# LayerNorm of the second row pair by ScalarE's square root, and another split of FFN1's blocks over the first two pairs

## The chip, the cores and the metric

The kernel runs on one core of one Trainium2 chip. The metric is the device time of one execution in microseconds. The kernel before takes 165.26 us, the median of 3 runs (164.93 to 165.86).

## The reference

The kernel adds two branches to its input. Both read the same LayerNorm of x. Branch A is a linear attention with softmax features, 16 heads of 28; branch B is a feed-forward net with SiLU.

```python
S, D, H, Dh, F = 2048, 448, 16, 28, 1792
xn = (x - mean(x)) / sqrt(var(x) + 1e-5)                    # per row
q, k, v = split_heads(xn @ wqkv)
pq, pk = q @ w_phi, k @ w_phi                                # per head, 28 x 28
phi_q = concat(softmax(pq), softmax(-pq)); phi_k = concat(softmax(pk), softmax(-pk))
kv = phi_k^T v;  z = sum over rows of phi_k
a = merge_heads((phi_q @ kv) / (phi_q . z + 1e-6)) @ wo
b = silu(xn @ w1) @ w2                                       # w1 448 x 1792, w2 1792 x 448
out = x + a + b
```

## The kernel before, in words

**Tiles.** The 2048 rows are 16 tiles of 128 rows, worked on in 8 pairs of tiles. A pair's normalised rows go through TensorE transposes into `xnT`, which every later matmul contracts over. FFN1 (`xn @ w1`, then SiLU) is cut into 14 blocks of 128 of the 1792 hidden columns.

**Who writes the order.** The program is a list of operations (`P.op`, `P.dma`) with their reads and writes. `schedule()` (lines 218 to 330) orders them per engine with planned durations, priorities and order-only edges (`odeps`). Each engine then runs its own list strictly in that order and waits on semaphores (`emit_engine`, line 1022). So an instruction that waits holds up all that stand behind it on its engine.

**LayerNorm.** `ln_stats` (589) takes mean and variance of a tile on VectorE. For pair 0, `ln_pair_first` (623) has ScalarE take the square root (629, tile `std`) and VectorE the reciprocal (632); `ln_norm` (601) normalises; `ln_tr` (610) transposes on TensorE and evicts PSUM to `xnT`, three of seven column blocks on ScalarE and four on VectorE. Between these stand warm-up matmuls on an identity matrix (528). For the other pairs, `ln_pair` (651) uses `ln_rstd` (595): VectorE adds epsilon (598) and GpSimd takes the power -0.5 (599); all seven blocks are evicted in one copy on VectorE (467). For pair 1 the two tiles have a power of their own each (`one_by_one`).

**ScalarE's tables.** The square root needs one table of functions, SiLU another. The compiler puts a table load ahead of the first instruction that needs another table.

**FFN1.** `ffn1_chunk(p0, npair, f0, fend, units)` (667) computes blocks f0 to fend for npair pairs that start at p0. One chunk fills two PSUM banks: four blocks of one pair (matmuls 128 wide) or two blocks of two pairs (256 wide). `contract` (472) makes two passes over each chunk: four steps of two matmuls that run side by side in the upper and lower half of the rows, then three steps with the halves exchanged; the second pass waits until the first is done. A chunk ends with a SiLU on ScalarE (688) that empties its two banks. `units` names the first bank of each chunk in turn; a chunk on banks that an earlier one used waits for that one's SiLU.

**The start.** Lines 737 to 764: pair 0's and pair 1's LayerNorm, blocks 0 to 10 of pair 0 alone (chunks of 4, 4, 3), pair 2's LayerNorm, the same blocks of pair 1 alone, pair 3's, then blocks 11 to 13 of both, pair 4's, and blocks of pairs 2 and 3 together. After FFN1 of six pairs and the folding of `w_phi` into the q and k weights come the k, v and q projections, the state kv, and the output with FFN2; FFN1 of pairs 6 and 7 fills in at a lower priority (963).

**Loads.** SP's queue carries, in order: x of tile 0, w1's first part, x of tiles 2 and 3, w1's second part (three transfers), w1's third part (three transfers, 557 to 562), x of pair 2, x of pair 3. The later loads are paced: x of tiles 8 to 11, wqkv and others each wait for one of the evictions to `xnT` (983 to 985).

Of the kernel before, what the change touches and what calls it, by code (L numbers as in the profile page):

```python
# [7 lines left out]
F32 = mybir.dt.float32  # L8
ACTF = mybir.ActivationFunctionType
# [323 lines left out]
def bass_parallel_sum__linear_kernel_hedgehog__dense_activation_silu__prompt_kernel(  # L333
# [13 lines left out]
    FT = FF // 128  # L347
# [7 lines left out]
    with es:  # L355
        def sb(name, shape, dt):
            return es.enter_context(nc.sbuf_tensor(name, shape, dt))
# [27 lines left out]
        ones4 = sb("ones4", [128, 4], F32)  # L385
        pre = sb("pre", [128, 2], F32)
        epsc = sb("epsc", [128, 1], F32)
        std = sb("std", [128, 2], F32)
        mtmp2 = sb("mtmp2", [128, 4], F32)
        mtmp3 = sb("mtmp3", [128, 4], F32)  # L390
        mask2 = sb("mask2", [128, 2], F32)
# [1 line left out]
        mv = sb("mv", [128, NT, 2], F32)  # L393
        ve = sb("ve", [128, NT], F32)
        neghalf = sb("neghalf", [128, NT], F32)
# [22 lines left out]
        P = _Prog()  # L418
# [43 lines left out]
        def act(dst, src, func, name, table=None, scale=1.0):  # L462
            return P.op("act", d_act(_cols(src)), lambda e: e.activation(dst, src, func, scale=scale),  # L463
                        reads=[src], writes=[dst], table=table, name=name)
# [7 lines left out]
        def contract(jobs, n, first, last, name, sync=None):  # L472
# [6 lines left out]
            for q, steps in enumerate(passes):  # L479
# [21 lines left out]
             reads=[ones_bf[:]], writes=[ident[:]], name="ident")  # L501
# [1 line left out]
        P.op("pool", d_pool(4), lambda e: e.memset(ones4[:], 1.0), writes=[ones4[:]], name="ones4")  # L503
        P.op("pool", d_pool(280, 0.9), lambda e: e.memset(BD[:], 0.0), writes=[BD[:]], name="bd0")
        P.op("pool", d_pool(1), lambda e: e.memset(epsc[:], EPS_LN), writes=[epsc[:]], name="eps")
        pre_op = act(pre[:, 0:1], neghalf[:, 0:1], ACTF.Sqrt, "pre", scale=-1.0)

        def late_constants():
            v4 = [a[:].rearrange("p (j h) -> p j h", j=2) for a in (ones4, mtmp2, mtmp3)]
# [16 lines left out]
             name="wopad")  # L526
# [14 lines left out]
        def load_x(t0, t1, eng="sp"):  # L541
            return load(x_sb[:, t0:t1, :], xt[:, t0:t1, :], (t1 - t0) * 128 * D * 2, f"x{t0}", eng)
# [17 lines left out]
        for c0, c1 in ((512, 1024), (1024, FF)):  # L560
            load_k(w1_sb, B_w1, c0, c1, "w1b")
            load_tail(w1_sb, B_w1, c0, c1, "w1bt")
        load_x(4, 6)
        load_x(6, 8)
        first_loads = len(P.ops)
        paced = []
# [34 lines left out]
        def ln_norm(p, t, eng="dve"):  # L601
            sl = p % NXN
            for c0, c1, o0 in (((0, D, 0),) if t % 2 == 0 else ((384, D, D), (0, 384, 512))):
                xn = xn_sb[:, sl, o0:o0 + c1 - c0]
                dur = 120 + (c1 - c0) * 0.6 if eng == "dve" else 120 + (c1 - c0) * 1.0
                P.op(eng, dur, lambda e, xn=xn, c0=c0, c1=c1: e.tensor_scalar(
                    xn, x_sb[:, t, c0:c1], mv[:, t, 0:1], rstd[:, t:t + 1], ALU.subtract, ALU.mult),
                    reads=[x_sb[:, t, c0:c1], mv[:, t, 0:1], rstd[:, t:t + 1]], writes=[xn], name="xn")
# [11 lines left out]
            else:  # L620
                copy_dve(dst, src, "xnT_ev", d_dve(128 * n, 2))

        def ln_pair_first(bk):
            for t in range(2):
                k = len(P.ops)
                ln_stats(t)
                if t:
                    P.ops[k].odeps.add(k - 2)
                P.op("act", 220, lambda e, t=t: e.activation(std[:, t:t + 1], mv[:, t, 1:2], ACTF.Sqrt, bias=epsc[:]),
                     reads=[mv[:, t, 1:2], epsc[:]], writes=[std[:, t:t + 1]], name="std")  # L630
            for t in range(2):
                P.op("dve", 150, lambda e, t=t: e.reciprocal(rstd[:, t:t + 1], std[:, t:t + 1]),
                     reads=[std[:, t:t + 1]], writes=[rstd[:, t:t + 1]], name="rstd")
                ln_norm(0, t)
            prev = None
            for n, js, eng in ((19, [0, 1, 2], "act"), (2, [3, 4, 5, 6], "dve")):
                k = len(P.ops)
                o = warm(n, 256)
                if prev:
                    P.ops[k].odeps.add(prev)  # L640
                k = len(P.ops)
                ln_tr(0, js, bk if eng == "act" else bk - 2, eng)
                P.ops[k].odeps.add(o.id)
                prev = P.ops[-1].id - 1
            ev = P.ops[-1]
            k = len(P.ops)
            o = warm(5, 256)
            P.ops[k].odeps.add(prev)
            return ev, o

        def ln_pair(p, one_by_one=False):
            t0, t1 = 2 * p, 2 * p + 1
            for t in (t0, t1):
                ln_stats(t)
                if one_by_one:
                    ln_rstd(t, t + 1)
            if not one_by_one:
                ln_rstd(t0, t1 + 1)
            ln_norm(p, t0)
            ln_norm(p, t1)  # L660
            ln_tr(p, [0, 1, 2, 3, 4, 5, 6], 6, "dve")

        silus = []
# [72 lines left out]

        last0, warm0 = ln_pair_first(6)
        k = len(P.ops)
        ln_pair(1, True)
        for o in P.ops[k:]:  # L740
            if o.eng == "dve":
                o.odeps.add(last0.id)
# [1 line left out]
        k = len(P.ops)  # L744
        ffn1_chunk(0, 1, 0, 4, (0, 2))
        P.ops[k].odeps.add(warm0.id)
        ffn1_chunk(0, 1, 4, 8, (0, 2))
        ffn1_chunk(0, 1, 8, 11, (0, 2))
        k = len(P.ops)
        ln_pair(2)  # L750
        for o in P.ops[k:]:
            if o.eng == "dve":
                o.odeps.add(last1)
        ffn1_chunk(1, 1, 0, 4)
        ffn1_chunk(1, 1, 4, 8)
        ffn1_chunk(1, 1, 8, 11)
        ln_pair(3)
        ffn1_chunk(0, 2, 11, FT)
        ln_pair(4)
        ffn1_chunk(2, 2, 0, 4)  # L760
        ln_pair(5)
# [219 lines left out]
            else:  # L981
                out_last(p)
        evs = [o.id for o in P.ops if o.name == "xnT_ev"]
        for o, d in zip(paced, evs[2:6]):
            o.deps.add(d)
        eks = [o.id for o in P.ops if o.name == "exp_k"]
        for o, d in zip(w2_loads + [wo_load], eks[0::2]):
# [112 lines left out]
```

## Time and profile before

| | us |
|---|---|
| median of 3 runs | 165.26 |
| lowest, highest | 164.93, 165.86 |
| the profiled execution | 165.84 |
| its span (first to last instruction) | 164.1 |
| TensorE busy / VectorE / ScalarE / GpSimd | 158.3 / 102.3 / 73.8 / 54.5 |
| granted TensorE clock | 1.0 all along |

The profile shows one execution. PE is TensorE's matmuls, PEld its weight loads, which run beside them; DVE is VectorE, ACT ScalarE, POOL GpSimd, SP SyncE. A row of a timeline has start, length, engine, line, operation, output and inputs, and how many like it were merged; in brackets stand the idle time of the engine ahead of it and what ended that. Matmuls are pipelined and their ends are modelled.

### The profile page before, as it was taken

The page shows a single profiled execution, that of the slowest core. Times are in us where ns is not written, and L with a number is a line of the kernel's source. Part 1 is how long each engine was busy: PE and PEld are TensorE (multiplying, and loading weights), DVE is VectorE, ACT ScalarE, POOL GpSimd, SP SyncE. Part 2 cuts the span into 40 slices and gives each one's busy share as a digit, 9 for nine tenths or more (in the row PEclk, how much of TensorE's full clock was granted, in tenths as well). Part 3 has the DMA queues.
Part 4 walks back from the last instruction along what each step waited for, and adds up shares of the span by engine and source line. Part 5 has one row for each costly group of instructions (what it writes and reads, how often), then busy time and mean ns, then how long its engine had stood idle before and what let it go on. Part 6 is the DMA issues. An engine that isn't in the chain of part 4 may idle for free.

```text
span 164.1 us, 5978 instructions
## 1 busy us (share of the span) xinstructions
PE 158.3 (96%) x2741; PEld 102.7 (63%) x2741; DVE 102.3 (62%) x185; ACT 73.8 (45%) x85; POOL 54.5 (33%) x79
## 2 busy tenths in 40 slices
PE   6999999999999999999999999999999999999994
PEld 4689799999754455545557865555555554455563
DVE  2859878932418887666878788578867865111211
ACT  3542756569688866786667562210220131200000
POOL 7021130110001777755574052553464265000000
PEclk9999999999999999999999999999999999999999
DMA  5974743000003332120000000010101010101011
GB/s 162 311 202 116 203 129 108 0 4 4 4 0 112 116 112 60 46 72 4 4 4 6 0 4 4 0 56 4 50 10 56 0 60 2 56 3 56 0 62 50
DMA packets 8197, 9.24 MB, mean 56 GB/s; under 512 B 1324, under 2 KB 7916, under 8 KB 8172
## 3 DMA queue, kind: packets, MB, share of 16 engines
q1 hardware_dynamic: 7868, 8.62, 17.1%
q8 instruction: 21, 0.34, 0.8%
q10 hardware_dynamic: 304, 0.25, 0.5%
q14 instruction: 4, 0.03, 0.1%
HBM read 7.02 MB, written 1.84 MB: 54 GB/s over the span
## 4 chain that ended last, share of the span: by engine, by line
PE 83%; DVE 7%; DMA 3%; ACT 2%; SPq 2%; issue 1%; DVEq 0%; ACTq 0%
PE psum L444 47%; PE psum L438 33%; PE psum L457 3%; DMA w_sb<-in_B_w_dram 3%; DVE scr L798 2%; SPq L536 2%; DVE wraw L901 1%; DVE Sk L795 1%; ACT oT L463 1%; ACT scr L463 1%; DVE den L892 1%; DVE KVZ L854 1%; DVE kvt L849 0%; DVE R L888 0%; DVE rden L895 0%
## 5 line engine op out<-in xcount | busy, mean ns | idle before, releaser
L444 PE MATMUL psum<-xnT,w_sb 64*128 64x256 bf16 (+1 forms) x938 | 49.4, 252 | 1.0 <-DMA w_sb<-in_B_w_dram 0.6
L438 PE MATMUL psum<-w_sb,hT 128*128 128x448 bf16 (+2 forms) x238 | 47.1, 342 | 0.0
L444 PEld LDWEIGHTS psum<-xnT,w_sb 64*128 64x128 bf16 x938 | 39.2, 94 | 5.4 <-PE psum L444 1.1
L463 ACT ACTIVATE hT<-psum 128x1024 bf16<-128x1024 f32 (+2 forms) x29 | 28.5, 995 | 21.7 <-PE psum L444 21.7
L438 PEld LDWEIGHTS psum<-w_sb,hT 128*128 128x128 bf16 x238 | 22.0, 98 | 18.9 <-issue 0.4
L798 POOL TENSOR_TENSOR scr<-scr,Rk 128x1792 bf16<-128x1792 bf16 (+1 forms) x8 | 24.2, 3021 | 22.8 <-DVE Rk L797 15.3
L920 POOL TENSOR_TENSOR xn_sb<-wraw 128x8 bf16<-128x8 f32 (+4 forms) x40 | 21.3, 564 | 30.1 <-DVE wraw L901 23.8
L941 DVE TENSOR_TENSOR out_sb<-psum,x_sb 128x448 bf16<-128x448 f32 (+2 forms) x17 | 10.1, 595 | 22.1 <-PE psum L438 22.1
L463 ACT ACTIVATE oT<-psum 128x896 bf16<-128x896 bf16 x8 | 7.3, 917 | 33.8 <-PE psum L457 28.3
L463 ACT ACTIVATE EqT<-psum 128x1024 bf16<-128x1024 f32 x16 | 15.5, 1021 | 8.4 <-PE psum L444 8.4
L901 DVE TENSOR_TENSOR wraw<-psum,Gq 128x1792 f32<-128x1792 f32 (+1 forms) x9 | 16.3, 1814 | 1.0 <-DVE Gq L896 0.5
L795 DVE TENSOR_REDUCE Sk<-scr 128x64 f32<-128x1792 bf16 (+1 forms) x9 | 16.2, 1811 | 1.1 <-ACT scr L463 0.5
L467 DVE CAST scr<-psum 128x896 bf16<-128x896 f32 x8 | 8.8, 1094 | 11.7 <-PE psum L444 11.7
L438 PE MATMUL psum<-wo_sb,oT 128*128 128x448 bf16 (+2 forms) x68 | 14.9, 342 | 0.1
L444 PE MATMUL psum<-xnT,wqk_sb 64*128 64x512 bf16 x112 | 14.8, 378 | 0.1
L463 ACT ACTIVATE scr<-psum 128x896 bf16<-128x896 f32 x16 | 13.8, 914 | 1.0
L599 POOL TENSOR_TENSOR rstd<-ve,neghalf 128x2 f32<-128x2 f32 (+1 forms) x8 | 5.3, 660 | 24.2 <-DVE ve L598 24.2
L444 PE MATMUL psum<-wqk_sb,xnT 64*128 64x448 bf16 x112 | 13.2, 349 | 0.0
L444 PE MATMUL psum<-wv_sb,xnT 64*128 64x448 bf16 x112 | 13.2, 349 | 0.0
L590 DVE BATCH_NORM_STATS2 st<-x_sb 128x6 f32<-128x448 bf16 x16 | 9.7, 613 | 3.6 <-DMA x_sb<-in_A_x_dram 3.6
L438 PEld LDWEIGHTS psum<-wo_sb,oT 128*128 128x128 bf16 x68 | 6.4, 98 | 5.9 <-ACT oT L463 0.5
L444 PEld LDWEIGHTS psum<-wqk_sb,xnT 64*128 64x128 bf16 x112 | 5.4, 94 | 5.4 <-ACT scr L463 0.2
(54 smaller groups left out, 120.1 us busy)
## 6 DMA issues: line engine op xcount, KB each, us to landing
out_dram<-out_sb SPq DMA_DIRECT2D x7, 224.0 KB, 2.0
w_sb<-in_B_w_dram SPq DMA_DIRECT2D x3, 448.0 KB, 3.3
x_sb<-in_A_x_dram SPq DMA_DIRECT2D x2, 448.0 KB, 3.4
w_sb<-in_B_w_dram SPq DMA_DIRECT2D x2, 384.0 KB, 4.7
x_sb<-in_A_x_dram SPq DMA_DIRECT2D x3, 224.0 KB, 5.7
wraw<-in_A_wqkv_dram SPq DMA_DIRECT2D x1, 672.0 KB, 4.3
w_sb<-in_B_w_dram SPq DMA_DIRECT2D x1, 576.0 KB, 6.4
wv_sb<-in_A_wqkv_dram SPq DMA_DIRECT2D x1, 336.0 KB, 4.0
```

The source lines that it names most:

```text
L438: lambda e: e.matmul(dst, lhsT, rhs, start=start, stop=stop, skip_group_check=True),
L444: r = e.matmul(dst, lhsT, rhs, start=start, stop=stop, skip_group_check=True)
L457: out = e.transpose(dst, src, ident[r, 64:128] if r == LO else ident[r, 0:64])
L463: return P.op("act", d_act(_cols(src)), lambda e: e.activation(dst, src, func, scale=scale), reads=[src], writes=[dst], table=table, name= ...
L467: return P.op("dve", dur, lambda e: e.tensor_copy(dst, src), reads=[src], writes=[dst], name=name)
L590: P.op("dve", 600, lambda e: e.bn_stats(st6[:, t, :], x_sb[:, t, :]), reads=[x_sb[:, t, :]], writes=[st6[:, t, :]], name="bnst")
L599: P.op("pool", 580, lambda e: e.tensor_tensor(r2, v2, nh, ALU.pow), reads=[v2, nh], writes=[r2], name="rstd")
L795: P.op("dve", d_dve(896 * n), lambda e, S4=S4, E4=E4: e.tensor_reduce(S4, E4, AXL.X, ALU.add), reads=[E4], writes=[S3], name="Sk")
L798: P.op("dve" if t0 else "pool", d_dve(896) if t0 else d_pool(896 * n, 1.57), lambda e, E4=E4, R4=R4, n=n: e.tensor_tensor(E4, E4, R4[:, :, ...
L901: P.op("dve", d_dve(896 * n), lambda e, dsto=dsto, U=U, G3=G3, n=n: e.tensor_tensor(dsto, U[:, :, :, 0:DH], G3[:, :, :, None].broadcast_to ...
L920: P.op("pool", d_pool(_cols(dst), 2.26), lambda e, dst=dst, a0=a0, a1=a1: e.tensor_tensor(dst, a0, a1, ALU.add), reads=[a0, a1], writes=[d ...
L941: P.op("dve", d_dve(c1 - c0), lambda e: e.tensor_tensor(dst, ob, xs, ALU.add), reads=[ob, xs], writes=[dst], name="out_ev")
```

## The change

Five edits. Line numbers of the changed kernel are some 1 to 7 higher.

- Pair 1's LayerNorm takes ScalarE's square root as pair 0's does (`ln_pair_sqrt`, which serves both), and its eviction is split: three blocks on ScalarE from banks 6 and 7, four on VectorE from banks 4 and 5.
- The square roots are marked with the table "sqrt" for the planner, and the first SiLU is ordered behind the last of them.
- FFN1's first blocks: 0 to 7 of pair 0 alone, 0 to 7 of pair 1 alone (its first chunk on banks 4 and 5, its second on banks 0 and 1), then 8 to 13 of both.
- x of pair 2 is loaded ahead of w1's third part.
- The pacing of later loads counts one eviction more, since pair 1 now has two.

In the built program, ScalarE's order becomes: pair 0's two roots and eviction, pair 1's two roots and eviction, the load of SiLU's table, the first SiLU. In TensorE's order, pair 1's transposes stand amid pair 0's second chunk, and the first matmul of pair 1's second chunk (which waits for pair 0's first SiLU) stands between the two passes of pair 1's first chunk.

```diff
-        std = sb("std", [128, 2], F32)
+        std = sb("std", [128, 4], F32)
...
-        pre_op = act(pre[:, 0:1], neghalf[:, 0:1], ACTF.Sqrt, "pre", scale=-1.0)
+        pre_op = act(pre[:, 0:1], neghalf[:, 0:1], ACTF.Sqrt, "pre", "sqrt", scale=-1.0)
...
             load_tail(w1_sb, B_w1, c0, c1, "w1bt")
-        load_x(4, 6)
+            if c0 == 512:
+                load_x(4, 6)
         load_x(6, 8)
...
-        def ln_pair_first(bk):
-            for t in range(2):
+        def ln_pair_sqrt(p):
+
+            for t in (2 * p, 2 * p + 1):
                 k = len(P.ops)
                 ln_stats(t)
-                if t:
+                if t % 2:
                     P.ops[k].odeps.add(k - 2)
                 P.op("act", 220, lambda e, t=t: e.activation(std[:, t:t + 1], mv[:, t, 1:2], ACTF.Sqrt, bias=epsc[:]),
-                     reads=[mv[:, t, 1:2], epsc[:]], writes=[std[:, t:t + 1]], name="std")
-            for t in range(2):
+                     reads=[mv[:, t, 1:2], epsc[:]], writes=[std[:, t:t + 1]], table="sqrt", name="std")
+            for t in (2 * p, 2 * p + 1):
                 P.op("dve", 150, lambda e, t=t: e.reciprocal(rstd[:, t:t + 1], std[:, t:t + 1]),
                      reads=[std[:, t:t + 1]], writes=[rstd[:, t:t + 1]], name="rstd")
-                ln_norm(0, t)
+                ln_norm(p, t)
+
+        def ln_pair_first(bk):
+            ln_pair_sqrt(0)
...
         last0, warm0 = ln_pair_first(6)
         k = len(P.ops)
-        ln_pair(1, True)
+        ln_pair_sqrt(1)
+        ln_tr(1, [0, 1, 2], 6, "act")
+        ln_tr(1, [3, 4, 5, 6], 4, "dve")
+        sqrt_last = [o.id for o in P.ops if o.name == "std"][-1]
...
         ffn1_chunk(0, 1, 0, 4, (0, 2))
         P.ops[k].odeps.add(warm0.id)
+        silus[0].odeps.add(sqrt_last)
         ffn1_chunk(0, 1, 4, 8, (0, 2))
-        ffn1_chunk(0, 1, 8, 11, (0, 2))
+        ffn1_chunk(1, 1, 0, 4, (4,))
+        ffn1_chunk(1, 1, 4, 8, (0,))
         k = len(P.ops)
         ln_pair(2)
...
-        ffn1_chunk(1, 1, 0, 4)
-        ffn1_chunk(1, 1, 4, 8)
-        ffn1_chunk(1, 1, 8, 11)
         ln_pair(3)
-        ffn1_chunk(0, 2, 11, FT)
+        ffn1_chunk(0, 2, 8, FT, (2, 4, 0))
         ln_pair(4)
...
-        for o, d in zip(paced, evs[2:6]):
+        for o, d in zip(paced, evs[3:7]):
             o.deps.add(d)
```

## The prediction

> **What bounds the kernel now.** I read the page first: the shares of busy time, the instruction queue of the DMA table and the chain that ended last.
>
> ```profile
> span 164.1 us, 5978 instructions
> PE 158.3 (96%) x2741; PEld 102.7 (63%) x2741; DVE 102.3 (62%) x185; ACT 73.8 (45%) x85; POOL 54.5 (33%) x79
> ...
> q8 instruction: 21, 0.34, 0.8%
> ...
> PE 83%; DVE 7%; DMA 3%; ACT 2%; SPq 2%; issue 1%; DVEq 0%; ACTq 0%
> ```
>
> TensorE is busy 158.3 of 164.1 us and holds 83% of the chain. The change acts between 7 and 20 us, so I asked for busy time by stage (columns: length, then busy time and count of PE, PEld, DVE, ACT, POOL, then clock, DMA share, GB/s).
>
> ```profile
> 6.88:8.25 1.37, 1.07 (x33) 0.90 (x34) 1.34 (x5) 0.59 (x1) 0.06 (x1) 1.00 0.98 318
> 8.92:16.55 7.63, 7.55 (x269) 7.21 (x270) 5.87 (x18) 2.86 (x3) 1.07 (x2) 1.00 0.50 138
> 18.63:31.00 12.37, 12.37 (x303) 11.61 (x301) 10.29 (x30) 7.21 (x8) 2.07 (x3) 1.00 0.43 132
> 54.00:82.40 28.40, 28.40 (x562) 15.24 (x564) 21.09 (x18) 20.57 (x24) 18.67 (x7) 1.00 0.20 60
> 82.40:97.80 15.40, 14.73 (x428) 10.86 (x426) 12.90 (x21) 10.20 (x11) 5.88 (x6) 1.00 0.01 4
> ```
>
> From 8.92 us on PE hardly rests: what it gains or loses in FFN1 goes through the stages behind it nearly one to one. A matmul's recorded end is modelled, so stops show better on the weight loads (PEld). These are the rows of its timeline from 8.88 us on that carry the argument; in brackets stands the idle time ahead of a row and what ended it.
>
> ```profile
> 8.88 1.15 PEld L444 LDWEIGHTS psum<-xnT,w_sb 64*128 64x128 bf16 x40 [0.47 <-DMA w_sb<-in_B_w_dram]
> 9.97 0.20 PEld L457 LDWEIGHTS psum<-ident,xn_sb 64*128 64x128 bf16 x6
> 10.09 0.31 PEld L444 LDWEIGHTS psum<-xnT,w_sb 64*128 64x128 bf16 x10
> ...
> 10.63 2.35 PEld L444 LDWEIGHTS psum<-xnT,w_sb 64*128 64x128 bf16 x79
> 13.23 1.73 PEld L444 LDWEIGHTS psum<-xnT,w_sb 64*128 64x128 bf16 x61 [0.25 <-issue]
> ...
> 16.96 0.28 PEld L444 LDWEIGHTS psum<-xnT,w_sb 64*128 64x128 bf16 x9 [0.29 <-issue]
> 17.48 0.94 PEld L444 LDWEIGHTS psum<-xnT,w_sb 64*128 64x128 bf16 x28 [0.24 <-PE psum L444]
> ...
> 22.33 2.62 PEld L444 LDWEIGHTS psum<-xnT,w_sb 64*128 64x128 bf16 x48
> ```
>
> Three stops stand there. The wait for w1's second part ends at about 8.9 us; the changed kernel's instructions and transfers up to it are the same. At 17.48 PE drains: the second pass of a chunk follows its first pass directly, which costs 0.24 us. At 13.23 and 16.96 it stops 0.25 and 0.29 us for nothing that the profile shows ("issue"). Between these two lie 128 weight loads in this timeline, so 256 PE instructions; the instruction queue moved 0.34 MB in 21 pieces, 16 KB each. I read the two stops as instruction blocks that come too late while 128-wide matmuls run. Another 128 loads on, near 22.3 us among 256-wide matmuls, there is no stop.
>
> Rates: (1.73 - 0.09) / 60 = 27 ns and (2.35 - 0.09) / 78 = 29 ns for a 128-wide matmul, I take 28; (2.62 - 0.09) / 47 = 54 ns for a 256-wide one (0.09 is one load). Two narrow ones (56) cost hardly more than a wide one.
>
> **The change part by part.**
>
> *Fewer narrow blocks.* Before, pairs 0 and 1 each do 11 of the 14 blocks alone (22 x 14 = 308 narrow matmuls) and 3 together (42 wide); after, 8 each (224) and 6 together (84). 84 x 28 = 2.35 us goes and 42 x 54 = 2.27 us comes: -0.08 us. There are 84 PE instructions fewer (weight loads included).
>
> *The square root for pair 1.* The trace has this path for pair 0, and pair 1's own path through GpSimd:
>
> ```profile
> 4.18 0.30 ACT L629 ACTIVATE std<-mv,epsc 128x1 f32<-128x1 f32 x1 [1.44 <-DVE mv L592]
> 5.35 0.26 PE L457 MATMUL psum<-ident,xn_sb 64*128 64x64 bf16 x6
> 5.68 0.49 ACT L463 ACTIVATE xnT<-psum 128x384 bf16<-128x384 bf16 x1 [0.54 <-PE psum L457]
> 6.19 1.28 ACT L463 ACT_TABLE_LOAD   x1
> 6.37 0.42 DVE L467 COPY xnT<-psum 128x512 bf16<-128x512 bf16 x1 [0.39 <-PE psum L457]
> ...
> 8.19 1.10 POOL L599 TENSOR_TENSOR rstd<-ve,neghalf 128x1 f32<-128x1 f32 x2 [3.83 <-DVE ve L598]
> 8.80 1.12 DVE L606 TENSOR_SCALAR xn_sb<-x_sb,mv,rstd 128x448 bf16<-128x448 bf16 x3 [0.34 <-POOL rstd L599]
> 9.97 1.02 ACT L463 ACTIVATE hT<-psum 128x1024 bf16<-128x1024 f32 x1 [2.50 <-PE psum L444]
> 10.78 0.62 DVE L467 COPY xnT<-psum 128x896 bf16<-128x896 bf16 x1 [0.87 <-PE psum L457]
> 11.77 1.15 DVE L590 BATCH_NORM_STATS2 st<-x_sb 128x6 f32<-128x448 bf16 x2 [0.36 <-DMA x_sb<-in_A_x_dram]
> ...
> 14.16 0.89 DVE L606 TENSOR_SCALAR xn_sb<-x_sb,mv,rstd 128x448 bf16<-128x448 bf16 x3
> ```
>
> Two roots of 0.30 us take the place of two GpSimd powers (1.10 us together); the normalised pair is ready at about 9.5 instead of 9.92 us. That buys nothing by itself: in PE's order 20 matmuls stand between 8.92 us and pair 1's first transposes, and pair 1's blocks now start behind all of pair 0's eight. Its place is off the path. What it costs is ScalarE's order. Before, the Silu table is loaded at 6.19 us in an idle stretch, and the first Silu starts at 9.97. After, the roots and an eviction of pair 1 stand ahead of the load, and the first Silu behind it:
> - pair 1's transposes start at 8.92 + 20 x 0.028 = 9.48 us; the eviction follows 0.33 us later, as at 5.35 and 5.68, and takes 0.49: 10.30.
> - table load, 0.02 + 1.28: 11.60. First Silu, 0.02 + 1.02: 12.64 instead of 10.99.
>
> Who waits for it: the second chunk of pair 1 takes the banks of pair 0's first chunk, and its first matmul stands in PE's queue amid pair 1's first chunk; 24 matmuls behind it need no Silu but must wait too. PE comes there after 6 + 14 + 10 + 10 + 10 + 24 + 32 = 106 matmuls (2.97 us), 14 transposes (by 9.97 to 10.09, 0.02 each: 0.28 at most, I take 0.20) and one unfilled pass change (0.24): 8.92 + 3.41 = 12.33 us. From an ACT end to PE's next start the chain has this row:
>
> ```profile
> 133.07 0.93 ACT oT L463
> 134.00 0.14 issue
> ```
>
> So PE goes on at 12.64 + 0.14 = 12.78 and **stands still 0.45 us**. The next Silus (13.7, 14.7) are ahead of PE's need (14.4 and later).
>
> *The pauses.* The first block border lies 11 matmul pairs behind this wait; a wait of 0.45 us ahead of it gives the late block more than the 0.25 us that it lacked, so I count that stop as gone. The next 128 loads hold 58 narrow and some 46 wide matmuls and last over 4 us instead of 3.7, so the second stop, 0.29, goes too. The bounds: both stay (0) or both go (-0.54). I take -0.54, because the border near 22.3 us shows no stop. The drain (0.24) is there once in either kernel: 0.
>
> The Trainium skill ("Runtime: NRT & Kernel Launch", Instruction fetch mechanics) says that instructions come in 16 KiB blocks of 256 and that the fetch is mostly hidden. The size agrees with the 0.34 MB in 21 pieces; the two stops speak against "hidden". By that page this term would be 0 and the sum +0.37.
>
> *x of pair 2 ahead of w1's third part.* 224 KB at the 318 GB/s above take 0.7 us. w1's third part, by these rows, lands near 10.5 us (the fourth of six issues from 2.23 on, some 0.6 each, and 6.4) and will land near 11.3; its first use is at 14.4: hidden by 3 us.
>
> ```profile
> 2.23 3.69 SPq L536 DMA_DIRECT2D w_sb<-in_B_w_dram  x6
> ...
> w_sb<-in_B_w_dram SPq DMA_DIRECT2D x1, 576.0 KB, 6.4
> ```
>
> Pair 2's statistics no longer wait until 11.77: they can start behind pair 1's copy: the last transposes start near 10.2, the copy some 0.3 us later, and it takes 0.42, so 10.9. In before 3.3 us pass from there to the end of the three normalisations (11.77 to 15.05), which gives 14.2; PE asks at 12.78 + 56 x 0.028 = 14.35. That is just hidden, and what it is short of would be added to PE. The paced loads hang on the same evictions, shifted by under a us; SP's queue has one place exchanged and nothing longer.
>
> *Later stages.* The order of work from the k stage on is the same but for one exchange of four matmul pairs. Block borders shift by 84 instructions against the work; a border that falls into a burst of the short k-v matmuls could cost a stop of the size seen, 0.25 to 0.29, or spare one: bounds of 0.29 either way. I take 0, since no row tells the sign.
>
> Sum: -0.08 + 0.45 - 0.54 = **-0.17 us**. The ends are +0.4 (both stops stay) and -0.6 (no wait for Silu). I round to -0.2: span 163.9. Around the span lay 165.84 - 164.1 = 1.7 us in the profiled execution, which is 0.6 above the median; against the median of 165.26 (runs from 164.93 to 165.86) the forecast is 165.05.
>
> **The rivals.**
> - *Nothing gained.* Stops stay, or the gain is lost between 82 and 98 us, where VectorE's chain and PE filler share the end (PE 14.73 of 15.40): 0 to +0.4, 165.3 to 165.7. For it: the chain's DVE share of 7%. Against: that stretch starts when the k stage ends, and PE is full up to there.
> - *ScalarE late: slower.* Each 0.1 us that the first Silu slips is 0.1 us of PE, from 12.33 us on. If a further stretch as long as the load follows it (1.28), the first Silu ends at 13.9, PE waits 1.7 us and the sum is +1.1: 166.4. It is slower than before from 0.17 us of slip on, and beyond 0.5% from 1.0 us on. For it: the load at 6.19 doesn't show the engine's restart, since the Silu waited for PE. Against it, the later load:
>
> ```profile
> 87.11 1.28 ACT L463 ACT_TABLE_LOAD   x1
> 88.40 1.02 ACT L463 ACTIVATE hT<-psum 128x1024 bf16<-128x1024 f32 x1
> ```
>
> The Silu starts 1.29 us after the load did. The Trainium skill ("ScalarE: Activation LUTs", What ACT_TABLE_LOAD costs) adds a drain of about 1.38 us to the 1283 ns of the load, which would give about this rival's time; the load agrees with 1.28, the drain doesn't show at 88.40.
> - *Clearly faster.* If the Silu wait is hidden (PE arrives later than I count) and every stop and the drain go: -0.08 - 0.54 - 0.24 = -0.86, 164.4. Against: the drain has no filler in the new order.
> - *The change doesn't do what it says.* The faster LayerNorm is real but unused; that is within my forecast.
>
> **How the numbers follow.** A measurement of this kernel can tell about 0.5%, 0.83 us. Chances: forecast (164.7 to 165.3) 0.5; nothing gained 0.27; ScalarE late 0.13; clearly faster 0.1, of which about 0.08 beyond 0.83 us. The late ScalarE alone is over +0.83, so slower 0.13, faster 0.08, same 0.79. The range, 164.4 to 165.8, leaves out the late ScalarE and a bit at the lower end.
>
> **What would show it.** Right: a table load at about 10.3 us with the first Silu near 11.6; a PE stop near 12.3 us of 0.3 to 0.6 us that ends with that Silu; no "issue" stop among FFN1's narrow matmuls; pair 2's statistics near 10.9. Wrong: PE waiting over 1 us there, PE waiting for xn_sb or for w1's third part, or new "issue" stops from 60 us on.

## The result, and the profile after

| | runs | median us | lowest to highest | ratio to before, 95% interval |
|---|---|---|---|---|
| before | 20 | 165.81 | 164.93 to 166.5 | |
| after | 20 | 165.06 | 164.47 to 165.73 | 0.9955 [0.9939, 0.9971] |
| before, second series | 22 | 166.04 | 165.37 to 166.39 | |
| after, beside the second series | 9 | 165.15 | 164.47 to 165.51 | 0.9942 [0.9923, 0.9962] |

The changed kernel is 0.75 us (the second time 0.9 us) faster; the forecast was 0.2. That its absolute number, 165.05, was met to 0.01 us is luck: it hung on the median of three runs of before (165.26), and with more runs that median is 165.8. Taken as a change, the result is where the forecast put its rival "clearly faster" (-0.86). What has to be explained is a gain about four times as large as the sum said.

The profiled execution of after took 164.47 us, as long as its fastest run; that of before took 165.84, its median. The two traces thus differ by more than the kernels do. The page of after, the lines that answer to those of before:

```profile
span 162.7 us, 5896 instructions
PE 157.2 (97%) x2699; PEld 101.8 (63%) x2699; DVE 102.0 (63%) x185; ACT 74.6 (46%) x87; POOL 53.4 (33%) x77
...
q8 instruction: 21, 0.34, 0.9%
...
PE 75%; DVE 7%; ACT 5%; issue 4%; DMA 3%; POOL 2%; SPq 2%; DVEq 0%
```

PE has 42 matmuls fewer (2741 to 2699), as counted. ScalarE's share of the chain went from 2% to 5%: the first SiLU is now on it. Its rows, from the second square root of pair 1 on:

```profile
8.68 0.29 ACT L631 ACTIVATE std<-mv,epsc 128x1 f32<-128x1 f32 x1 [0.43 <-DVE mv L593]
9.41 0.49 ACT L463 ACTIVATE xnT<-psum 128x384 bf16<-128x384 bf16 x1 [0.44 <-PE psum L457]
9.92 1.28 ACT L463 ACT_TABLE_LOAD   x1
11.21 3.05 ACT L463 ACTIVATE hT<-psum 128x1024 bf16<-128x1024 f32 x3
```

And PE's weight loads from w1's second part on:

```profile
8.49 0.59 PEld L444 LDWEIGHTS psum<-xnT,w_sb 64*128 64x128 bf16 x20 [0.35 <-DMA w_sb<-in_B_w_dram]
...
10.47 1.56 PEld L444 LDWEIGHTS psum<-xnT,w_sb 64*128 64x128 bf16 x56 [0.24 <-PE psum L444]
12.29 1.56 PEld L444 LDWEIGHTS psum<-xnT,w_sb 64*128 64x128 bf16 x56 [0.25 <-ACT hT L463]
13.81 0.21 PEld L457 LDWEIGHTS psum<-ident,xn_sb 64*128 64x128 bf16 x8
13.96 0.90 PEld L444 LDWEIGHTS psum<-xnT,w_sb 64*128 64x128 bf16 x28
```

Two stops are left, the unfilled pass change at 10.47 and the SiLU at 12.29, and no "issue" stop. The order of things is the one forecast. VectorE's rows show pair 2's statistics at 10.54 (forecast 10.9, before 11.77) and its normalised rows from 13.14 on; the transposes at 13.81 don't wait:

```profile
10.54 0.62 DVE L591 BATCH_NORM_STATS2 st<-x_sb 128x6 f32<-128x448 bf16 x1
...
13.14 0.89 DVE L607 TENSOR_SCALAR xn_sb<-x_sb,mv,rstd 128x448 bf16<-128x448 bf16 x3
```

**The same kernel, another execution.** A second profile of after, of 165.39 us, has the same instructions in the same order and other stops:

```profile
10.38 1.56 PEld L444 LDWEIGHTS psum<-xnT,w_sb 64*128 64x128 bf16 x56 [0.24 <-PE psum L444]
12.26 0.67 PEld L444 LDWEIGHTS psum<-xnT,w_sb 64*128 64x128 bf16 x24 [0.32 <-ACT hT L463]
13.46 0.93 PEld L444 LDWEIGHTS psum<-xnT,w_sb 64*128 64x128 bf16 x32 [0.53 <-issue]
...
26.08 0.37 PEld L457 LDWEIGHTS psum<-ident,wraw 64*128 64x128 bf16 x20 [0.48 <-DVE xnT L467]
```

An "issue" stop of 0.53 us is there after all, and a wait of 0.48 us for VectorE at 26.08. So one trace doesn't show what this kernel does; the median lies between the two.

Where the time went, by stretch (ends are first instructions in the traces; the fold is the first matmul on `BD`):

| stretch, us | before | after, 164.47 | after, 165.39 |
|---|---|---|---|
| start to the first FFN1 matmul | 6.89 | 7.01 | 6.98 |
| to the fold | 26.76 | 25.48 | 26.43 |
| to the first matmul of the state kv | 24.59 | 24.61 | 24.60 |
| to `kvt` (VectorE reads the state) | 31.81 | 31.65 | 31.65 |
| to the end | 74.05 | 74.00 | 74.00 |
| span | 164.10 | 162.75 | 163.66 |

In the second stretch PE's stops add up. Waits for w1's second part: 0.94 us before, 0.42 and 0.42 after. Stops of 0.06 us and more from there to 33 us: 1.26 before, 0.60 and 1.57 after. Fewer narrow blocks: -0.08. Sums: -0.52 - 0.66 - 0.08 = -1.26 (the table says -1.28) and -0.52 + 0.31 - 0.08 = -0.29 (-0.33).

The first of these terms is not the change's. w1's second part landed at 8.78 us in before and at 8.39 and 8.36 in after, but over all profiles of this study anywhere from 7.77 to 8.79, in kernels whose transfers up to it are the same. PE's waits for it are luck, up to half a microsecond either way in a single trace.

A gain of 0.16 us stands in the fourth stretch in both profiles. It is one VectorE operation on the path to the state, of the same shape; its row in before and in after, each with the GpSimd operation of the same line that runs beside it (it works on the other tile of the pair):

```profile
86.67 2.63 DVE L798 TENSOR_TENSOR scr<-scr,Rk 128x896 bf16<-128x896 bf16 x1
...
86.66 1.70 POOL L798 TENSOR_TENSOR scr<-scr,Rk 128x896 bf16<-128x896 bf16 x1 [1.63 <-DVE Rk L797]
```

```profile
85.53 2.48 DVE L805 TENSOR_TENSOR scr<-scr,Rk 128x896 bf16<-128x896 bf16 x1
...
85.36 1.70 POOL L805 TENSOR_TENSOR scr<-scr,Rk 128x896 bf16<-128x896 bf16 x1 [1.60 <-DVE Rk L804]
```

VectorE's operation took 2.63 us in before and in the kernel below with x alone moved, 2.53 in three others, 2.48 in nine. In all 14 profiles it ends 0.95 us after GpSimd's, whichever of the three lengths it has. So what moved is GpSimd's start: 0.23 us after the end of the reciprocal that it needs in before (86.66 - 86.43), 0.08 us in after (85.36 - 85.28), 0.13 in the three others. No edit names that operation, and why its start differs between the programs stays open.

### The profile page after: what moved, and what is told of

Same layout as the page of the kernel before. It is cut to its first block, busy times and chain, and to the rows that moved or that the text cites. A ratio compares the mean times of both kernels' runs of the same rounds, so it can differ in the third digit from the quotient of the medians.

```text
span 162.7 us, 5896 instructions
## 1 busy us (share of the span) xinstructions
PE 157.2 (97%) x2699; PEld 101.8 (63%) x2699; DVE 102.0 (63%) x185; ACT 74.6 (46%) x87; POOL 53.4 (33%) x77
## 4 chain that ended last, share of the span: by engine, by line
PE 75%; DVE 7%; ACT 5%; issue 4%; DMA 3%; POOL 2%; SPq 2%; DVEq 0%
PE psum L444 42%; PE psum L438 30%; DMA w_sb<-in_B_w_dram 3%; PE psum L457 3%; ACT scr L463 2%; POOL xn_sb L927 2%; ACT L463 2%; DVE scr L805 2%; SPq L536 2%; DVE wraw L908 1%; DVE Sk L802 1%; DVE den L899 1%; ACT hT L463 1%; ACT oT L463 1%; DVE KVZ L861 1%
## 5 line engine op out<-in xcount | busy, mean ns | idle before, releaser
L444 PE MATMUL psum<-xnT,w_sb 64*128 64x256 bf16 (+1 forms) x896 | 48.5, 256 | 0.4 <-DMA w_sb<-in_B_w_dram 0.2
L444 PEld LDWEIGHTS psum<-xnT,w_sb 64*128 64x128 bf16 x896 | 38.4, 94 | 4.7 <-PE psum L444 0.8
L463 ACT ACTIVATE hT<-psum 128x1024 bf16<-128x1024 f32 x28 | 28.3, 1024 | 16.9 <-PE psum L444 14.2
L438 PE MATMUL psum<-wo_sb,oT 128*128 128x448 bf16 (+2 forms) x68 | 14.9, 342 | 0.1
L463 ACT ACTIVATE scr<-psum 128x896 bf16<-128x896 f32 x16 | 13.8, 914 | 1.4 <-PE psum L444 0.7
L600 POOL TENSOR_TENSOR rstd<-ve,neghalf 128x2 f32<-128x2 f32 x6 | 4.2, 694 | 23.7 <-DVE ve L599 23.7
```

The lines of the kernel that those rows point to most:

```text
L438: lambda e: e.matmul(dst, lhsT, rhs, start=start, stop=stop, skip_group_check=True),
L444: r = e.matmul(dst, lhsT, rhs, start=start, stop=stop, skip_group_check=True)
L600: P.op("pool", 580, lambda e: e.tensor_tensor(r2, v2, nh, ALU.pow), reads=[v2, nh], writes=[r2], name="rstd")
```

## The experiments

Theory A: TensorE's instructions come in blocks of 128 weight loads, and a block can be used some 2.5 us after its fetch began. A border is met at a fixed count of instructions (the first of those that matter here after 221 weight loads in before, after 222 in the kernels with the new split, which have one or two semaphore instructions fewer on PE's queue ahead of it), so what an edit saves ahead of it is given back there unless PE arrives later than the block; a stop ahead of it costs little, since the fetch runs on meanwhile. The rival, the forecast's own way of adding: each stop has its price and each edit its term.

| kernel | against before | median us | runs | ratio, 95% interval |
|---|---|---|---|---|
| x_only | x of pair 2 early | 165.8 | 12 | 0.9994 [0.9966, 1.0023] |
| blocks_only | 8, 8, 6 split | 165.5 | 12 | 0.9971 [0.9945, 0.9997] |
| ln_only | pair 1's root and split eviction | 165.98 | 12 | 1.0009 [0.9984, 1.0035] |
| ln_blocks | all but x early | 165.48 | 12 | 0.9978 [0.9953, 1.0002] |
| blocks_x | all but pair 1's root and eviction | 165.1 | 12 | 0.9974 [0.9954, 0.9995] |
| pow_split | all, but pair 1's power on GpSimd | 164.96 | 12 | 0.9953 [0.9935, 0.9972] |
| banks67 | all, pair 1's second chunk on other banks | 166.42 | 12 | 1.0043 [1.0015, 1.0072] |
| id_first | all, first SiLU ahead of the table load | 164.96 | 6 | 0.9933 [0.9911, 0.9956] |
| slip | all, table load 0.5 us later | 165.23 | 8 | 0.9956 [0.9936, 0.9976] |
| slip3 | all, table load 1.7 us later | 165.39 | 12 | 0.9968 [0.9953, 0.9982] |

Each ratio is to runs of before made beside it: median 165.83 for the first four kernels, 165.72 for the next three, 166.04 for the last three.

### x of pair 2 alone (x_only)

```diff
             load_tail(w1_sb, B_w1, c0, c1, "w1bt")
-        load_x(4, 6)
+            if c0 == 512:
+                load_x(4, 6)
         load_x(6, 8)
```

> The kernel before with one edit: x of pair 2 is loaded ahead of w1's third part. Theory A (the gain comes from PE's stops among narrow matmuls, above all the two issue stops): the order of PE is unchanged, the stops near 13.2 and 17.0 us stay with 0.25 to 0.29 us each, the time is the kernel before's, 0 +- 0.2 us. Theory B (the gain comes from the loads: w1's second part, which landed at 8.4 instead of 8.8 us in the changed kernel's trace, lands earlier because x stands behind it in the queue): PE's first long wait ends near 8.4 us and the time falls by 0.3 to 0.5 us.

No gain: 0.9994. In its profile w1's second part landed 0.92 us earlier than in before's (7.86), and yet the fold came 0.12 us later. PE's rows at the borders:

```profile
16.81 0.28 PEld L444 LDWEIGHTS psum<-xnT,w_sb 64*128 64x128 bf16 x9 [0.56 <-issue]
17.32 0.94 PEld L444 LDWEIGHTS psum<-xnT,w_sb 64*128 64x128 bf16 x28 [0.24 <-PE psum L444]
...
22.55 1.53 PEld L444 LDWEIGHTS psum<-xnT,w_sb 64*128 64x128 bf16 x29 [0.28 <-issue]
```

At the first border PE stops 0.10 us (12.80), too short for a bracket in this view. The stop that was 0.29 us at 16.96 is 0.56 at 16.81: PE comes earlier and waits longer, and passes the border at nearly the same time (the packets began at 14.37 here, at 14.38 in before). It even stops at the next one, among wide matmuls, where before did not. What had been won ahead of the borders was lost at them and in two waits of 0.2 us for pair 1's rows. The earlier landing is not due to the move: it comes as early in kernels that load x as before does (7.89 in the next one).

### The split of the blocks alone (blocks_only)

```diff
-        ffn1_chunk(0, 1, 8, 11, (0, 2))
+        ffn1_chunk(1, 1, 0, 4, (4,))
+        ffn1_chunk(1, 1, 4, 8, (0,))
...
-        ffn1_chunk(1, 1, 0, 4)
-        ffn1_chunk(1, 1, 4, 8)
-        ffn1_chunk(1, 1, 8, 11)
         ln_pair(3)
-        ffn1_chunk(0, 2, 11, FT)
+        ffn1_chunk(0, 2, 8, FT, (2, 4, 0))
```

> The kernel before with one edit: 8 blocks of pair 0, 8 of pair 1, 6 of both; LayerNorm of pair 1 and the loads as before. Theory A: no Silu wait, the table is loaded at 6.2 us; the first issue stop stays (0.25), the second goes because wide matmuls follow: 0.3 to 0.6 us faster than before, unless PE comes to pair 2's transposes before its x (landed 11.7) is normalised. Theory B (LayerNorm and loads make the gain): no gain, 0 +- 0.2.

About half of the whole gain, 0.9971 (some 0.5 us, as theory A had it; theory B's "no gain" lies at the edge of the interval), though its profiled execution (165.93) lies above its median. That one has a large stop at the first border (rows of its weight loads):

```profile
11.45 1.57 PEld L444 LDWEIGHTS psum<-xnT,w_sb 64*128 64x128 bf16 x56 [0.25 <-DVE xnT L467]
13.87 1.89 PEld L444 LDWEIGHTS psum<-xnT,w_sb 64*128 64x128 bf16 x62 [0.85 <-issue]
```

The records of the instruction queue say why: the block's packet began at 11.29 us, in before at 10.73, and PE went on 2.58 us after it (13.87 - 11.29; before 13.23 - 10.73 = 2.50).

### LayerNorm of pair 1 alone (ln_only)

```diff
-        ln_pair(1, True)
+        ln_pair_sqrt(1)
+        ln_tr(1, [0, 1, 2], 6, "act")
+        ln_tr(1, [3, 4, 5, 6], 4, "dve")
...
+        silus[0].odeps.add(sqrt_last)
```

> The kernel before with one edit: pair 1's LayerNorm by ScalarE's root and split eviction; blocks 11 + 11 + 3 and loads as before. Theory A: the first Silu starts at 11.2 to 11.6 us instead of 10.0; pair 0's third chunk takes the first one's banks and is reached near 11.1, so PE stops there for 1.0 to 1.3 us; the first issue stop is absorbed by it: 0.3 to 0.9 us slower than before. Theory B (the earlier LayerNorm is worth something by itself): 0.1 to 0.4 us faster.

No gain, and no loss that can be told (1.0009); both expectations missed. Theory A had 1.0 to 1.3 us for the SiLU's stop. It is small again, 0.17 us; pair 2's late x and a later SiLU cost more:

```profile
12.50 1.51 PEld L444 LDWEIGHTS psum<-xnT,w_sb 64*128 64x128 bf16 x54 [0.17 <-ACT hT L463]
14.58 0.31 PEld L457 LDWEIGHTS psum<-ident,xn_sb 64*128 64x128 bf16 x8 [0.57 <-DVE xn_sb L606]
...
18.99 1.10 PEld L444 LDWEIGHTS psum<-xnT,w_sb 64*128 64x128 bf16 x22 [0.70 <-ACT hT L463]
```

### Without x of pair 2 early (ln_blocks)

```diff
-            if c0 == 512:
-                load_x(4, 6)
+        load_x(4, 6)
```

(against the changed kernel)

> The changed kernel without its load edit: x of pair 2 again behind w1's third part. PE's order is that of the changed kernel. Theory A: the PE stops of the narrow stage are those of the changed kernel, but pair 2's statistics start near 11.8 instead of 10.5 us and its transposes, wanted at 13.8, wait 0.5 to 1.0 us for xn_sb: 0 to 0.4 us faster than before instead of 0.75. Rival (the load edit buys nothing, as the forecast's cover of 0.15 us would have it): 0.6 to 0.8 us faster than before.

0.9978: some 0.4 us of the changed kernel's gain is missing, though the intervals overlap. The profile shows the wait that the move takes away:

```profile
12.22 1.59 PEld L444 LDWEIGHTS psum<-xnT,w_sb 64*128 64x128 bf16 x56 [0.16 <-ACT hT L463]
14.18 0.31 PEld L457 LDWEIGHTS psum<-ident,xn_sb 64*128 64x128 bf16 x8 [0.36 <-DVE xn_sb L606]
```

Pair 2's rows come 0.36 us late here. So the move is worth nothing alone and about this wait once the split lets PE ask for pair 2 at 13.8 us instead of 14.9 (the transposes' start in before's trace).

### Twice as many warm-ups, half as wide (warm38)

```diff
-                o = warm(n, 256)
+                o = warm(2 * n, 128) if n == 19 else warm(n, 256)
```

> The kernel before with its first 19 warm-up matmuls of 256 columns as 38 of 128 columns: 19 weight loads (and 38 PE instructions) more ahead of FFN1, PE's later order the same. Theory A (the issue stops stand at the borders of instruction blocks, 256 instructions or 128 loads apart): they come again after 221, 349 (and perhaps 477) weight loads, counted from the start, which is 19 loads earlier in FFN1's work; so the row of loads that ends at the first stop, 79 in the kernel before, has 60, or the border is passed without a stop if the block came in time (2.5 us after its fetch began). Rival (the stops belong to a place in the work, such as a change of pass): they stay between the same two matmuls, after 240 and 368 loads.

The warm-up's work is the same, its instructions are 19 more, and the stop moves with the count:

```profile
10.28 1.78 PEld L444 LDWEIGHTS psum<-xnT,w_sb 64*128 64x128 bf16 x60
13.82 2.23 PEld L444 LDWEIGHTS psum<-xnT,w_sb 64*128 64x128 bf16 x80 [1.76 <-issue]
```

It stands after 221 weight loads of the program, as in before, and not after the 240 that would be the same place in the work. The block's packet began at 11.22 us, and PE went on 2.60 us later. The time, of one run, was 166.59 us. The stop belongs to the count of instructions; with this the reading of "issue" as a block border is shown.

### Without pair 1's root and eviction (blocks_x)

```diff
-        ln_pair_sqrt(1)
-        ln_tr(1, [0, 1, 2], 6, "act")
-        ln_tr(1, [3, 4, 5, 6], 4, "dve")
+        ln_pair(1, True)
...
-        silus[0].odeps.add(sqrt_last)
```

(against the changed kernel)

> The changed kernel with pair 1's old LayerNorm (GpSimd's power, one copy on VectorE); new blocks and early x of pair 2. Theory A: the Silu table is loaded at 6.2 us and nothing waits for the first Silu; instead the block border after 221 loads stops PE until 2.5 us after the fetch began, 0.3 to 0.8 us; with pair 2's x early, the rest is as in the changed kernel: 0.3 to 0.7 us faster than before, within 0.3 us of the changed kernel. Rival (the earlier LayerNorm itself makes the gain): not faster than blocks_only's 0.33 us.

```profile
11.45 3.46 PEld L444 LDWEIGHTS psum<-xnT,w_sb 64*128 64x128 bf16 x118 [0.25 <-DVE xnT L467]
...
19.16 1.87 PEld L444 LDWEIGHTS psum<-xnT,w_sb 64*128 64x128 bf16 x36 [0.34 <-PE psum L444]
24.08 0.14 PEld L457 LDWEIGHTS psum<-ident,xn_sb 64*128 64x128 bf16 x6 [0.23 <-DVE xn_sb L607]
```

0.9974: faster than before by some 0.4 us, and the changed kernel's 0.75 lies within the interval, as does blocks_only's gain; so neither expectation is settled. The SiLU's stop is gone, and a wait of the same 0.25 us for VectorE's copy of all seven blocks stands in its place; a pass change of 0.34 and a wait of 0.23 us follow. The border stop that theory A had named did not come: the block's packet began at 10.10, and PE came 2.87 us later.

### The power on GpSimd, the split eviction kept (pow_split)

```diff
-        ln_pair_sqrt(1)
+        for t in (2, 3):
+            ln_stats(t)
+            ln_rstd(t, t + 1)
+        ln_norm(1, 2)
+        ln_norm(1, 3)
         ln_tr(1, [0, 1, 2], 6, "act")
```

(against the changed kernel)

> The changed kernel with GpSimd's power for pair 1 but the split eviction kept (three blocks on ScalarE, four on VectorE): the Silu table is loaded at 6.2 us, the first Silu starts at about 9.6, pair 1's ScalarE eviction stands behind it. Theory A: no Silu stop; a border stop after 221 loads of up to 0.5 us; pair 1's first chunk may wait for the eviction behind the first Silu (ready near 11.2): 0.4 to 0.9 us faster than before, the same as the changed kernel within 0.3. Rival (the root on ScalarE is what counts): at least 0.3 us slower than the changed kernel.

0.9953, the same as the changed kernel (the intervals leave room for 0.4 us). ScalarE's square root isn't what most of the gain comes from. The profiled execution, 166.2, lies at the upper end of its runs (164.62 to 166.2), with the border again:

```profile
14.01 1.93 PEld L444 LDWEIGHTS psum<-xnT,w_sb 64*128 64x128 bf16 x62 [1.09 <-issue]
```

No SiLU wait ahead of it, a fetch that began at 11.53, and a stop of 1.09 us (theory A: up to 0.5) that ends 2.48 us later.

### Other banks for pair 1's second chunk (banks67)

```diff
-        ffn1_chunk(1, 1, 4, 8, (0,))
+        ffn1_chunk(1, 1, 4, 8, (6,))
```

(against the changed kernel)

> The changed kernel with pair 1's second chunk on banks 6 and 7 instead of 0 and 1: its first matmul no longer waits for the first Silu (the planner places pair 2's transposes later, since they share these banks). Theory A (the Silu stop only fills the time in which the next instruction block is fetched): the stop at 12.3 us goes, a shorter one of up to 0.25 us appears after 221 loads near 12.8 us, and the time is the changed kernel's within 0.25 us: 0.5 to 0.95 us faster than before. Rival (the Silu stop costs its full 0.25 us on top): 0.25 us faster than the changed kernel, no stop after 221 loads.

Slower, 1.0043, which neither expectation had. The SiLU's stop is gone (166 loads in one row from 10.34), and at the border stands a stop of 0.09 us (12.66, 2.54 us after its packet began; too short for a bracket), as theory A had it. But the planner's order changed with the banks, and SP's queue, on which the paced loads wait for evictions, ran later. Its rows:

```profile
18.02 4.70 SPq L536 DMA_DIRECT2D BD<-in_A_w_phi_dram  x6
22.76 0.37 SPq L536 DMA_DIRECT2D x_sb<-in_A_x_dram  x1
```

In after x of tiles 8 to 11 was issued at 19.62; here at 22.76. VectorE waits for it 1.42 us, and PE for VectorE:

```profile
27.98 0.37 PEld L457 LDWEIGHTS psum<-ident,wraw 64*128 64x128 bf16 x20 [1.35 <-DVE scr L467]
```

The profiled execution took 165.65 us, and this kernel's runs go from 165.31 to 167.59. So what makes its slower executions, and with them the median, is not in this trace, and the time does not decide between the two expectations.

### The changed kernel again (after_again)

> The changed kernel once more, unchanged, as the measure for the three beside it. Both theories: within 0.3 us of its 165.06. In the trace, by theory A (a block of 128 weight loads can be used some 2.5 us after its fetch began), the PE order alone does not fix the stops: the fetch begins at another time in each execution, so the sum of the stops from 8.9 to 33 us may differ by 0.3 us from that of the earlier profile (some 0.6 us) with the same instructions.

165.15, and the other stops shown above: 1.57 us instead of 0.60 with the same instructions, more than the 0.3 us of difference that had been expected. The block's packet began at 10.90 us here and at 10.32 in the first profile; PE passed the border 2.56 and 2.60 us later, with a stop in the one and with none in the other. The wait at 26.08 also has an issue behind it. SP's row of this profile, and that of the first:

```profile
20.14 1.55 SPq L536 DMA_DIRECT2D x_sb<-in_A_x_dram  x1
```

```profile
19.62 0.38 SPq L536 DMA_DIRECT2D x_sb<-in_A_x_dram  x1
```

The issue took 1.55 us instead of 0.38; the transfer landed at 24.86 instead of 23.08, and VectorE, which had waited for it 0.56 us, copied `xnT` later.

### The first SiLU ahead of the table load (id_first)

```diff
-                o = act(dst, src, ACTF.Silu, "silu", table="silu")
+                o = act(dst, src, ACTF.Silu if silus else ACTF.Identity, "silu", table="silu")
```

(against the changed kernel)

> The changed kernel with its first SiLU eviction as a plain copy (function Identity; so pair 0's blocks 0 to 3 have no SiLU). It no longer stands behind the table load: load and first SiLU change places, the PE order stays. The stop of PE that ended with the first SiLU (0.25 us at 12.29) must go. Theory A: the border after 221 weight loads is then reached 0.25 us earlier, before its block is usable, and a stop named issue takes its place: time within 0.15 us of the changed kernel's. Rival (the Silu stop is a loss of its own): 0.25 us faster, with no stop near 12.8.

```profile
9.81 0.49 ACT L463 ACTIVATE xnT<-psum 128x384 bf16<-128x384 bf16 x1 [0.70 <-PE psum L457]
10.20 1.02 ACT L463 ACTIVATE hT<-psum 128x1024 bf16<-128x1024 f32 x1
11.23 1.28 ACT L463 ACT_TABLE_LOAD   x1
```

```profile
12.56 1.51 PEld L444 LDWEIGHTS psum<-xnT,w_sb 64*128 64x128 bf16 x54 [0.18 <-PE psum L444]
```

The wait for the SiLU is gone, and PE stops at the same place for 0.18 us: the pass change of pair 1's first chunk. In the changed kernel one pair of matmuls stands between the two passes, and it is that pair that waits for the SiLU; while it waits, the first pass drains. So of the stop of 0.25 us only about 0.07 seems to be the SiLU's own (0.14 of the 0.32 in the second profile). Theory A had named another successor, a stop at the border, and that didn't come (border 13.14, its packet 10.38: 2.76 us, enough). The time, 164.96, is 0.19 below the changed kernel's beside it, with intervals that overlap widely.

### A later table load (slip, slip3)

```diff
+        slip = P.op("act", 1.0, lambda e: e.activation(
+            hT[:, 12:14, :, 7, 0:112], x_sb[:, 2, :].rearrange("p (a b c) -> p a b c", a=2, b=2), ACTF.Identity, scale=1.0),
...
+        silus[0].odeps.add(slip.id)
```

(against the changed kernel; slip3 has three of them in a row)

> The changed kernel with one more ScalarE copy of 128 x 448 (about 0.5 us, its output used by nobody) ahead of the Silu table load. The first SiLU ends near 12.75 instead of 12.25. The forecast's rival priced each 0.1 us of slip at 0.1 us of PE: the stop at 12.3 grows from 0.25 to about 0.75 us and the time by 0.5 us, to about 165.55. Theory A says the same, since the border is already met without a stop in the changed kernel and nothing is left to cover. Other rival: a later wait has slack and swallows it, growth under 0.2 us.

> The same with three such copies (about 1.3 to 1.5 us). By the price of 0.1 us for 0.1 us: a stop of about 1.6 us at 12.3, time 1.3 to 1.5 us above the changed kernel's, some 166.5, which is where the forecast put its rival of the late ScalarE (166.4). If a later wait swallows part of it: under 1.0 us.

One copy moves the load to 10.39, by 0.47 us, and PE's stop grows by 0.29 to 0.36:

```profile
12.76 1.57 PEld L444 LDWEIGHTS psum<-xnT,w_sb 64*128 64x128 bf16 x56 [0.61 <-ACT hT L463]
...
25.78 0.37 PEld L457 LDWEIGHTS psum<-ident,wraw 64*128 64x128 bf16 x20 [0.25 <-DVE xnT L467]
```

But the time grows by 0.08 us, not by 0.5. Against the second profile of after, 0.29 us more at the SiLU is matched by 0.53 us less at the border (no stop; its packet began at 10.01 and PE came at 13.39) and 0.23 less at the wait for VectorE. Three copies cost 0.24 us where 1.3 to 1.5 were expected:

```profile
9.80 1.78 ACT L755 ACTIVATE hT<-x_sb 128x448 bf16<-128x448 bf16 x3
11.60 1.28 ACT L463 ACT_TABLE_LOAD   x1
12.89 2.85 ACT L463 ACTIVATE hT<-psum 128x1024 bf16<-128x1024 f32 x3
```

```profile
12.38 0.67 PEld L444 LDWEIGHTS psum<-xnT,w_sb 64*128 64x128 bf16 x24 [0.24 <-PE psum L444]
13.97 0.90 PEld L444 LDWEIGHTS psum<-xnT,w_sb 64*128 64x128 bf16 x32 [0.92 <-ACT hT L463]
```

Here the planner, which knew of the three operations, put the 24 matmuls of the second pass ahead of the pair that waits, so its 1.7 us of slip are 1.16 us of stops, and neither the border nor VectorE stops PE behind them. For one copy the spread of the runs allows a cost of up to some 0.5 us, so its price alone doesn't decide; for three the forecast's price is ruled out, for that order of PE.

## Why the prediction was right or wrong

*Bound.* Right: from 8.9 us on what PE stops is what counts, and the stages from the fold on take the same time but for 0.2 us. "The same up to w1's second part" holds for the instructions, not for the clock: the landing moved by up to a microsecond between profiles (7.77 to 8.79), more than any term of the sum.

*Fewer narrow blocks.* -0.08 and 42 matmuls: nothing contradicts it, and it is too small to be seen alone.

*The SiLU stop.* The mechanism was right in every step: table load 1.4 us after PE's start on w1's second part (9.92 - 8.49; forecast 10.30 - 8.92 = 1.38), the first SiLU's end 3.75 us after it (forecast 3.72), PE's wait for it. The size was too large, 0.45 against 0.25 and 0.32. In the first profile PE came at 12.04 (12.29 - 0.25), 3.55 us after that start and not 3.41, and went on 0.05 us after the SiLU's end, not the 0.14 taken from a row of another stage. And the step "the drain (0.24) is there once in either kernel: 0" missed that before has a second, half-filled pass change (0.13 us at 20.39, too short for a bracket) and that after has one of its own, which hides in this very stop; id_first shows it as 0.18 us when the stop is taken away. The term's own cost was about 0.1 us, not 0.45.

The Trainium skill ("ScalarE: Activation LUTs", What ACT_TABLE_LOAD costs) adds a drain of about 1.38 us to the load. No run shows it: the load starts 0.02 us after the operation ahead of it ends, and SiLU follows the load's start at 9.92 + 1.29, 10.39 + 1.29 and 11.60 + 1.29 us.

*The pauses.* -0.54 was right in kind: the two stops are block borders (warm38), and the wait ahead of the first gives the late block its time (it did in the first profile of after; in the second the block's packet began 0.58 us later, and PE stopped 0.53 us all the same). It was taken as certain, and it isn't: the fetch began between 9.98 and 11.53 us over the profiles, and the same kernel passed the border once without a stop and once with 0.53. The Trainium skill ("Runtime: NRT & Kernel Launch", Instruction fetch mechanics) calls the fetch mostly hidden; here it costs up to 1.76 us at narrow matmuls, and at wide ones once 0.28 (x_only, 22.55).

*x of pair 2.* "That is just hidden" was right (no wait at 13.81). Entering it as 0 was not: without it the other edits run into 0.36 us of waiting for pair 2, so the sum had a benefit in it that no term named. By itself the move gains nothing (x_only); beside the split it takes that wait away, and the times agree with this, though their intervals overlap.

*Later stages.* Forecast 0 within 0.29 either way; measured -0.2, of it 0.16 in the start of one GpSimd operation, for a reason left open. What was not foreseen is at 26 us: an earlier PE meets the load of tiles 8 to 11, and waits 0.25 to 0.48 us in five of the eight profiles in which that issue takes 1.4 us or more. It gives back part of the gain.

*The rivals.* The late ScalarE was overpriced: "each 0.1 us that the first Silu slips is 0.1 us of PE" is right for the stop (0.47 us of slip: 0.36 more of stop, and PE 0.11 later) and too dear for the time, as slip3 shows for its order of PE. "Nothing gained" is out. "Clearly faster" had the size of the change, -0.86, but not its terms: it took the SiLU's wait as hidden and both pauses and the drain as gone, and the drain stayed (0.24 us at 10.47).

In sum, forecast -0.2, measured -0.75 to -0.9. The terms that make the difference, as far as the runs tell: SiLU's stop 0.13 to 0.2 us shorter than forecast, the late stage 0.2, and two stops of before that after doesn't have, the half-filled pass change and this wait, 0.3 together:

```profile
28.09 0.09 PEld L457 LDWEIGHTS psum<-ident,wraw 64*128 64x128 bf16 x1 [0.19 <-DVE scr L467]
```

This wait, 0.19 to 0.20 us, is in the profiles of all six kernels that keep GpSimd's power for pair 1, and of those with the root only in banks67's, where it is the 1.35 us above; whether the root removes it was not tried. From these terms goes what the border and the wait at 26 us cost in the mean. How large that last mean is can't be read from two profiles, so the split stays rough. What the runs bear best: the split of the blocks alone has half the gain or more (0.9971, with the 0.15 us of the VectorE operation in it); the early x and the split eviction add to it only in its company (x_only, ln_only), by amounts whose intervals overlap; and the square root adds nothing that can be told (pow_split), so that the last rival, an unused LayerNorm, fits that edit.

## What to carry to other kernels

Price a new wait by what stands behind it until the next place where PE has to wait anyway: as id_first and the slips suggest, a stop just ahead of an instruction-block border, a pass change or a late transfer costs only what it exceeds these by. Count PE's instructions, not only its time, where matmuls are short: the borders lie at fixed counts, and an edit ahead of one gains nothing if PE then comes before the block. And where executions of one kernel differ by 0.6%, take terms from two profiles before believing a tenth of a microsecond.

## What was not expected of the hardware

- A block of 128 weight loads and their matmuls was usable 2.44 to 2.61 us after its packet on the instruction queue began, in the eight stops of this kind over 0.15 us (in six kernels); three shorter ones, of 0.07 to 0.10 us, ended 2.35 to 2.76 us after it. The packet began when PE was between 129 and 192 loads into the program, for the border at 221 or 222; what sets this was not found.
- One DMA issue on SP's queue, of 448 KB, took 0.36 to 0.38 us in six profiles and 1.39 to 1.73 us in eight, and its transfer landed 3.4 to 4.4 and 4.4 to 5.0 us after its start; which of the two came differed between executions of one kernel.
- A VectorE operation of one shape took 2.48, 2.53 or 2.63 us, according to the program, beside a GpSimd operation of 1.70 us. In all 14 profiles its length is 0.95 us and the time in which both run (1.53, 1.58 or 1.68 us); in the two profiles of after it was the same.
